# Moving VectorE sums within a fused attention and feed-forward kernel: T4's sums beside batch 1's product with B22, and the sums of w_in spread over the last batch's first products

## The chip, the cores and the metric

One core of one Trainium2 chip. The metric is the device time of one execution in microseconds, here the median of several runs. All runs quoted were fast, with a granted TensorE clock of 0.997 to 1.0. The profile's span is some 1.8 to 2 us shorter than that time; both are given where they are compared.

Engines: PE is TensorE (PEld its weight loads), DVE is VectorE, ACT is ScalarE, SP issues the transfers. A line of the timeline reads: start and length in us, engine, line of the kernel, operation, result<-inputs, shapes, and how many instructions it merges; brackets give the idle time just before it and who ended it. In a list of waits the three numbers are the sum in us, how often, and the longest.

## The reference

```python
def _attn_ref(x, state):                      # x (8, 8, 512, 64), state (8, 8, 32, 64)
    scores = scale * x @ state.T; a = softmax(scores);   xread = a @ state
    scores2 = scale * state @ x.T; a2 = softmax(scores2); sread = a2 @ x
    return concatenate([xread, sread], axis=2)
def _moe_ref(x, w_in, w_out):                 # x: the result above as (4352, 512) tokens
    h = x @ w_in                              # (4352, 2048)
    g = h * (1.0 / (1.0 + np.exp(-1.702 * h)))
    return g @ w_out                          # (4352, 512)
```

(Shortened, the softmax as words.) The 512 x-rows of each of 8 batches are one block of work; the 32 state rows of all batches are gathered and done last, as a block called sr.

## The kernel before

From batch 1 on, the product g @ w_out is done in Strassen's form: seven half-size products in place of eight, at the price of sums and differences on DVE. T1, T2, T3, T4 are differences of the quarters of w_out. Where there is room, some of the seven are split once more, into seven products of eight recorded matmuls each. Each batch carries "hooks": lists of other work (attention of the next batch, sums) that are issued at named places between the products.

One batch, cut to what the argument touches:

```python
product(bank(0), A_of(0, 0), B11, "P1")        # hooks P1a, P1b between and after its halves
... # q1, q2, q4
product(bank(1), A_of(0, 1), B21, "P2")        # hooks P2a, P2b
tt(osb, bank(1), k1); out(0, 0, osb)           # first output block; frees bank 1
... # four subtracts, one correction, hook P2
product(bank(0), S1, T1, "P5")                 # hooks P5a, P5b
strassen_low(..., low2, low_banks(), k2, ...)  # P6: seven small products with T2, hooks P6.1 ...
left3 = sums(0, ...); tt(t01, bank(0), k2)
hook("P6")
left4 = sums(NU, ...)                          # (not in batch 1)
product(bank(3), A_of(0, 1), B22, "P3")        # the product with B22, hooks P3a, P3b
strassen_low(left3, ..., low3, ...)            # P7: seven small products with T3
strassen_low(left4, ..., low4, ...)            # P4: seven small products with T4
                                               # (batch 1: one whole product with T4)
```

Inside the small form three PSUM banks are used in turn, so a product must wait until the add of the product three places earlier has read its bank:

```python
product(o[0], a11, b11);  nc.scalar.copy(p, o[0]);  at(1)
product(o[1], s2, t2);    add(u2, o[1], p);         at(2)
product(o[2], a12, b21);  add(c11, o[2], p);        at(3)
product(o[0], a21, t3);   add(u3, o[0], u2);        at(4)
product(o[1], s1, t1);    ...                       # fifth: needs u2's read of o[1]
```

After batch 1 the sums of T4 were made once and stored, to be loaded by later batches; and the last batch's hooks made the sums for sr (eight of 1024 columns over w_in, four of 256 over the state rows), one per hook:

```python
hooks = {name: [steps[k]] for k, name in enumerate(
    ("P1b", "P2a", "P2", "P5a", "P5b", "P6", "P3a", "P3b", "P7.1", "P7.2", "P7.3", "P7.4"))}
hooks["P3b"].append((low_third, (T2,)))        # restores T2 (gives back a quarter that the small form had turned into a difference); likewise T3 at P4.1, T4 at P4.7
...
strassen_two(b, out_of(b), hooks, a4)
if b == 1:
    t = low4_room()
    for fn, args in low_sums(T4, low4_parts(t)):
        fn(*args)                              # three subtracts of 512 columns
    nc.sync.dma_start(kept4, t)
    low_third(T4)                              # a fourth, in place
```

## Time and profile before

| | before |
|---|---|
| time, median | 738.25 us (738.12 to 738.28, 3 runs) |
| span of the profile | 736.3 us |
| PE busy | 720.9 us (98%) |
| DVE busy | 539.4 us (73%) |
| waits of PE for DVE where the change works | 1.6 us (last batch) and 0.6 us (after batch 1) |

The columns are: window in us, its length, then busy us (and instructions) of PE, PEld, DVE, ACT and POOL, PE's granted clock, DMA share and GB/s.

```profile
155.00:203.00 48.00, 48.00 (x403) 40.59 (x402) 37.47 (x76) 14.40 (x29) 0.00 (x0) 1.00 0.06 23
203.00:240.00 37.00, 36.42 (x176) 31.86 (x175) 23.32 (x38) 12.51 (x20) 0.00 (x0) 1.00 0.28 74
240.00:631.00 391.00, 391.00 (x2860) 340.10 (x2859) 291.41 (x597) 128.68 (x238) 0.00 (x0) 1.00 0.13 36
631.00:660.00 29.00, 29.00 (x163) 26.28 (x162) 21.04 (x33) 2.89 (x6) 0.00 (x0) 1.00 0.11 37
660.00:690.00 30.00, 28.37 (x224) 27.35 (x224) 22.35 (x53) 2.45 (x8) 0.00 (x0) 1.00 0.08 28
```

From 155 to 690 us PE is busy for the whole of every stretch but two: 37.00 - 36.42 = 0.58 us are missing after batch 1, and 30.00 - 28.37 = 1.63 us in the last batch. Between them, over 391 us, nothing is missing.

### The profile page before, as it was taken

The numbers are of one execution on the slowest core, as the hardware profiler recorded it, in microseconds if no ns is written. First come the engines' busy times: TensorE is split into PE (matmuls) and PEld (weight loads), VectorE is DVE, ScalarE is ACT, GpSimd is POOL, SyncE is SP. The second block draws the span as 40 slices with busy tenths as digits, with TensorE's granted clock in tenths as the row PEclk, the third lists the DMA queues.
The fourth block names the chain that finished last, engine by engine and source line by source line (L and its number), as shares of the span: only waits on it lengthen the run. The fifth ranks groups of instructions, "written<-read, shape, count | busy, mean of one in ns | idle before, by whom it ended". The sixth has DMA issues, their size and how long they took to land.

```text
span 736.3 us, 11509 instructions
## 1 busy us (share of the span) xinstructions
PE 720.9 (98%) x4757; PEld 567.4 (77%) x4759; DVE 539.4 (73%) x1077; ACT 233.8 (32%) x430; POOL 0.8 (0%) x8
## 2 busy tenths in 40 slices
PE   7999999999999999999999999999999999999996
PEld 3333444478888789879888789878987988898995
DVE  6997999729766887668867786688667886778440
ACT  4786411033224511432144323341144214200210
POOL 0000000000000000000000000000000000000000
PEclk9999999999999999999999999999999999999999
DMA  9921244010041011300140014001120010010000
GB/s 234 344 93 52 89 162 125 0 58 15 1 121 27 16 35 54 60 1 16 46 102 1 16 45 105 0 16 45 50 55 1 15 62 26 1 58 29 16 1 28
DMA packets 49780, 40.84 MB, mean 55 GB/s; under 512 B 36544, under 2 KB 44224, under 8 KB 49728
## 3 DMA queue, kind: packets, MB, share of 16 engines
q1 hardware_dynamic: 49728, 40.11, 18.5%
q8 instruction: 37, 0.61, 0.3%
q14 instruction: 15, 0.12, 0.1%
HBM read 30.41 MB, written 9.70 MB: 54 GB/s over the span
## 4 chain that ended last, share of the span: by engine, by line
PE 93%; DVE 2%; ACT 2%; DMA 2%; issue 0%; SPq 0%; DVEq 0%; ACTq 0%
PE o L670 27%; PE o L938 16%; PE low L622 10%; PE o L490 8%; PE h L472 7%; PE o L622 6%; PE upx L938 5%; PE M L303 4%; PE o L533 2%; PE xT L282 2%; PE o L303 1%; PE sr L452 1%; PE warm L123 1%; PE upx_sr L938 1%; DMA out_dram<-osb_sr 1%; PE eT L441 1%
## 5 line engine op out<-in xcount | busy, mean ns | idle before, releaser
L670 PE MATMUL o<-w_out,g 128*128 128x256 f32 x672 | 152.7, 381 | 0.0
L948 DVE TENSOR_TENSOR g<-o,g 128x512 f32<-128x512 f32 (+1 forms) x140 | 88.0, 650 | 84.3 <-PE o L938 83.4
L670 PEld LDWEIGHTS o<-w_out,g 128*128 128x128 f32 x672 | 125.2, 190 | 26.2 <-issue 10.5
L945 ACT ACTIVATE g<-g 128x512 f32<-128x512 f32 (+1 forms) x84 | 49.8, 599 | 101.3 <-DVE g L948 101.3
L938 PE MATMUL o<-ta,M 128*128 128x256 f32 x192 | 49.4, 380 | 0.6 <-DVE g L948 0.6
L670 PE MATMUL o<-sums,later 128*128 128x256 f32 x224 | 49.5, 379 | 0.0
L938 PE MATMUL upx<-aT,M 128*128 128x256 f32 x192 | 49.3, 379 | 0.0
L938 PE MATMUL o<-ta,ms 128*128 128x256 f32 x192 | 48.3, 379 | 0.0
L670 PEld LDWEIGHTS o<-sums,later 128*128 128x128 f32 x224 | 42.6, 190 | 5.8
L432 ACT COPY M<-M 128x512 f32<-128x512 f32 x64 | 33.2, 597 | 37.7 <-PE M L303 37.7
L938 PEld LDWEIGHTS o<-ta,M 128*128 128x128 f32 x192 | 36.4, 190 | 5.9 <-DVE g L948 1.0
L938 PEld LDWEIGHTS o<-ta,ms 128*128 128x128 f32 x192 | 36.5, 190 | 5.0
L938 PEld LDWEIGHTS upx<-aT,M 128*128 128x128 f32 x192 | 36.1, 190 | 4.7
L513 DVE TENSOR_TENSOR later<-g,g 128x512 f32<-128x512 f32 (+1 forms) x32 | 20.8, 649 | 17.5 <-ACT g L475 17.5
L303 PE MATMUL M<-w_in,stT 64*32 64x512 f32 x512 | 32.7, 594 | 0.2 <-ACT eT L442 0.2
L622 PE MATMUL low<-low,g 128*128 128x128 f32 x256 | 32.8, 275 | 0.0
L472 PE MATMUL h<-low,M 128*128 128x512 f32 x64 | 29.7, 600 | 1.4 <-DVE low L384 1.4
L622 PEld LDWEIGHTS low<-low,g 128*128 128x128 f32 x256 | 30.7, 192 | 0.0
L629 ACT COPY pu<-o 128x128 f32<-128x128 f32 x13 | 3.4, 265 | 84.6 <-PE o L622 84.6
L472 PE MATMUL h<-aT,M 128*128 128x512 f32 x64 | 28.7, 599 | 1.4 <-ACT M L432 1.4
L625 DVE TENSOR_TENSOR pu<-low,pu 128x128 f32<-128x128 f32 x27 | 7.8, 290 | 29.1 <-PE low L622 29.1
L490 PE MATMUL o<-w_out,g 128*128 128x512 f32 x64 | 28.7, 594 | 0.0
(186 smaller groups left out, 1187.8 us busy)
## 6 DMA issues: line engine op xcount, KB each, us to landing
later<-in_moe_w_out_dram SPq DMA_DIRECT2D x16, 512.0 KB
xn<-in_x_dram SPq DMA_DIRECT2D x28, 256.0 KB
w_out<-in_moe_w_in_dram SPq DMA_DIRECT2D x12, 512.0 KB
low<-low SPq DMA_DIRECT2D x7, 768.0 KB
out_dram<-osb SPq DMA_DIRECT2D x18, 256.0 KB
out_dram<-later SPq DMA_DIRECT2D x14, 256.0 KB
later<-in_moe_w_in_dram SPq DMA_DIRECT2D x4, 512.0 KB
sums<-in_x_dram SPq DMA_DIRECT2D x4, 256.0 KB
```

The costliest lines, as they stand in the source:

```text
L282: nc.tensor.transpose(ps[:, c], x_heads(b, c, j), ident)
L303: nc.tensor.matmul(ps[g][st], A[b]["stT"][rows, st], rhs(rows, j), start=True, stop=True)
L432: nc.scalar.copy(m[:, g], ps[g])
L472: nc.tensor.matmul(hps, lhs[i], rhs[i], start=(i == 0), stop=(i == n - 1))
L490: nc.tensor.matmul(ops, G[key, f // 2][:, f % 2, P * r : P * (r + 1)], w_out[:, f], start=(f == 0), stop=(f == NF - 1))
L513: nc.vector.tensor_tensor(out=s1, in0=a21, in1=a22, op=ALU.add)
L533: nc.tensor.matmul(ps[:, r], lhs[f][:, P * r : P * (r + 1)], rhs[:, f], start=(first and r == 0 and f == 0), stop=(f == HF - 1), skip_grou ...
L622: nc.tensor.matmul(ps, lhs[f], rhs[:, f], start=(f == 0), stop=(f == QF - 1))
L670: nc.tensor.matmul(ps[:, r], lhs[f][:, P * r : P * (r + 1)], rhs[:, f], start=(r == 0 and f == 0), stop=(f == HF - 1), skip_group_check=True,)
L938: nc.tensor.matmul(ps[:, k], lhs[i][:, o : o + P], rhs[i], start=(first and k == 0 and i == 0), stop=(i == n - 1), skip_group_check=True,)
L945: nc.scalar.activation(out=dst, in_=src, func=AF.Gelu_apprx_sigmoid)
L948: nc.vector.tensor_tensor(out=dst, in0=ps, in1=x, op=ALU.add)
```

## The change

Its intent: take DVE work out of the two places where PE waits for DVE, and put it where DVE has idle time. Part A moves T4's three sums to hook P3a of batch 1. Part B deals the twelve sums for sr out anew, seven of the eight long ones ahead of P6, and restores T2 at hook P6.

```diff
+    def low4_make(a):
+        t = low4_room()
+        for fn, args in low_sums(T4, low4_parts(t)):
+            fn(*args)
+        nc.sync.dma_start(kept4, t)
...
-            hooks = {
-                name: [steps[k]]
-                for k, name in enumerate(("P1b", "P2a", "P2", "P5a", "P5b", "P6", "P3a", "P3b", "P7.1", ...))
-            }
-            hooks["P3b"].append((low_third, (T2,)))
+            order = (
+                ("P1b", 1), ("P2a", 4), ("P2", 1), ("P5a", 1), ("P3a", 1), ("P7.1", 1), ("P7.2", 1), ("P7.3", 1), ("P7.4", 1),
+            )
+            ...
+            for name, t in (("P6", T2), ("P4.1", T3), ("P4.7", T4)):
+                hooks[name] = [(low_third, (t,))]
...
+        hooks["P3a"][k:k] = [(low4_load if b > 1 else low4_make, (a4,))]
+        strassen_two(b, out_of(b), hooks, a4 if b > 1 else None)
         if b == 1:
-            t = low4_room()
-            for fn, args in low_sums(T4, low4_parts(t)):
-                fn(*args)
-            nc.sync.dma_start(kept4, t)
             low_third(T4)
```

More of the change, by code (lines that the diff above doesn't have):

```diff
@@ L1130 @@
             steps, left, right = sr_sums()
-            hooks = {
-                name: [steps[k]]
-                for k, name in enumerate(("P1b", "P2a", "P2", "P5a", "P5b", "P6", "P3a", "P3b", "P7.1", "P7.2", "P7.3", "P7.4"))
-            }
-            hooks["P3b"].append((low_third, (T2,)))
-            hooks["P4.1"] = [(low_third, (T3,))]
-            hooks["P4.7"] = [(low_third, (T4,))]
+            order = (
+                ("P1b", 1), ("P2a", 4), ("P2", 1), ("P5a", 1), ("P3a", 1), ("P7.1", 1), ("P7.2", 1), ("P7.3", 1), ("P7.4", 1),
+            )
+            hooks = {}
+            for name, n in order:
+                hooks[name], steps = steps[:n], steps[n:]
+            assert not steps
+            for name, t in (("P6", T2), ("P4.1", T3), ("P4.7", T4)):
+                hooks[name] = [(low_third, (t,))]
         for name, first in ahead.items():
             hooks[name] = first + hooks.get(name, [])
-        a4 = None
-        if b > 1:
-            a4 = {}
-            hooks["P3a"] = hooks.get("P3a", [])
-            k = 3 if b + 1 < B else 0
-            hooks["P3a"].insert(k, (low4_load, (a4,)))
-        strassen_two(b, out_of(b), hooks, a4)
+        a4 = {}
+        k = 3 if b + 1 < B else 0
+        hooks["P3a"][k:k] = [(low4_load if b > 1 else low4_make, (a4,))]
+        strassen_two(b, out_of(b), hooks, a4 if b > 1 else None)
         if b == 1:
-            t = low4_room()
-            for fn, args in low_sums(T4, low4_parts(t)):
-                fn(*args)
-            nc.sync.dma_start(kept4, t)
             low_third(T4)
```

## The prediction

> **What bounds the kernel now.** I read the page first (busy shares, then the chain that ended last), then the list of waits of TensorE alone, then the order of time of PE and DVE around each wait that the change could touch.
>
> ```profile
> span 736.3 us, 11509 instructions
> ...
> PE 720.9 (98%) x4757; PEld 567.4 (77%) x4759; DVE 539.4 (73%) x1077; ACT 233.8 (32%) x430; POOL 0.8 (0%) x8
> ...
> PE 93%; DVE 2%; ACT 2%; DMA 2%; issue 0%; SPq 0%; DVEq 0%; ACTq 0%
> ```
>
> The reader is to see that TensorE (PE) is busy for 98% of the span and makes 93% of the chain. The change removes no matmul, so only PE's holes can shrink: 736.3 - 720.9 = 15.4 us, most of them in the start and the last stores. The list of waits says which holes belong to VectorE (DVE):
>
> ```profile
> PE low L622 <- DVE pu L625: 1.6, 1, 1.6
> PE h L472 <- DVE low L384: 1.4, 1, 1.4
> ...
> PE o L938 <- DVE g L948: 0.6, 1, 0.6
> ```
>
> Two of these lie where the diff works (the L384 one is in the attention prologue). The larger, in order of time on PE and on DVE in the last batch:
>
> ```profile
> 668.61 1.06 PE L622 MATMUL o<-w_out,g 128*128 128x128 f32 x8
> 669.50 1.06 PE L622 MATMUL low<-w_out,g 128*128 128x128 f32 x8
> 672.20 1.16 PE L622 MATMUL low<-low,later 128*128 128x128 f32 x8 [1.63 <-DVE pu L625]
> ```
>
> ```profile
> 655.72 0.29 DVE L625 TENSOR_TENSOR pu<-low,pu 128x128 f32<-128x128 f32 x1 [1.47 <-PE low L622]
> ...
> 664.59 1.22 DVE L901 TENSOR_TENSOR ws<-ws,w_in 128x1024 f32<-128x1024 f32 x1
> ...
> 668.65 1.22 DVE L901 TENSOR_TENSOR w_in<-w_in,w_in 128x1024 f32<-128x1024 f32 x1
> 669.78 1.22 DVE L901 TENSOR_TENSOR ws<-w_in,ws 128x1024 f32<-128x1024 f32 x1
> 670.92 0.68 DVE L1080 TENSOR_TENSOR sums<-sums 128x512 f32<-128x512 f32 x1
> 671.52 0.42 DVE L901 TENSOR_TENSOR ta_sr<-srT 128x256 f32<-128x256 f32 x1
> 671.86 0.28 DVE L625 TENSOR_TENSOR pu<-low,pu 128x128 f32<-128x128 f32 x1
> ```
>
> Seven products of eight small matmuls (P7) follow the product with B22 (P3). The fifth rewrites the PSUM bank of the second, so it needs the small add of 671.86. That add's input was ready near 668.9, but DVE first works off w_in sums, T2's restoring subtract and one srT sum. Earlier, at 655.72, DVE had stood idle for 1.47 us: room in the wrong place. The smaller hole, after batch 1 (DVE):
>
> ```profile
> 195.26 0.69 DVE L837 TENSOR_TENSOR ms<-M 128x512 f32<-128x512 f32 x1 [1.17 <-ACT M L432]
> ...
> 199.59 0.29 DVE L625 TENSOR_TENSOR pu<-low,pu 128x128 f32<-128x128 f32 x1 [2.92 <-PE low L622]
> ...
> 211.51 0.68 DVE L1080 TENSOR_TENSOR low<-sums 128x512 f32<-128x512 f32 x1
> 212.22 1.42 DVE L1080 TENSOR_TENSOR low<-sums,low 128x512 f32<-128x512 f32 x2
> 213.56 0.68 DVE L1080 TENSOR_TENSOR sums<-sums 128x512 f32<-128x512 f32 x1
> 214.16 0.68 DVE L948 TENSOR_TENSOR g<-o,g 128x512 f32<-128x512 f32 x1
> ```
>
> Four operations on T4 stand ahead of the first add of batch 2's up projection; PE resumes at 214.90. Beside P3, at 192 to 199, DVE has 1.17 + 2.92 us idle.
>
> **What the Trainium skill says.** "VectorE: DVE Perf Modes", section on the TRN2 errata of SBUF-source operations, gives an fp32 tensor_tensor of N columns (N+151)/0.96 ns: 1224 for 1024 columns, 691 for 512, 424 for 256, 291 for 128. The trace agrees: 1216 to 1219, 680 to 693, 412 to 425, 287 to 291. So a moved sum costs what it cost before. The same page, "Two Vector instructions with no wait between them", says an instruction that is not held starts before its predecessor is through; here neighbours start 1.13 us apart at 1024 columns and 0.60 at 512, and I count with these distances. "PSUM — Partial Sum Buffer", "Engine vs sequencer instructions", calls VectorE's queue strict FIFO; the 671.86 add, ready since 668.9 and run in turn, agrees. Position in the queue is therefore the whole effect. The same page's rule on bank collisions (guard a bank by semaphores) is why the fifth product must wait for that read.
>
> **The change, part by part.** Each engine has as many instructions as before. PE's and ACT's order is unchanged; only DVE's order changes, and one DMA moves.
>
> Part A, T4 after batch 1. Three subtracts (211.51 to 213.56, 2.05 us) and the store of their result move beside P3, behind the transposes that end near 192.5. There DVE then does 2.05 us of T4, 1.57 of the four ta sums, 1.4 of the two ms sums: 5.0 of the 7.06 us until 199.59. P7's first add is not late, by 2.0 us. At 211.51 only T4's restoring subtract is left (0.60), so DVE is free at 212.1; the add can then start when its product is through. In batch 3 that add starts 2.00 us after the first up matmuls (292.99 against 290.99), here 210.70 + 2.00 = 212.7 instead of 214.16. What PE gains: in batch 3 the product that had to wait starts 294.45 - 290.99 = 3.46 us after the first up matmuls; in batch 2, 214.90 - 210.70 = 4.20. Gain 0.74 us, somewhat more than the idle figure of 0.58, because the restarted matmul is longer too.
>
> Part B, w_in sums in the last batch. Before, five of the eight 1024-column sums precede P6 (the seven small products ahead of P3), one follows it and two stand beside P3. After, seven precede P6 and one follows. Ahead of P6: from 645.60, four sums at 1.13 (s2, hi, s4, s1) bring the first output add from 647.02 to 650.1; it must have freed its bank by 653.67, when P6 begins there: 2.9 us to spare with its 0.7. Then 2.53 us of add, subtracts and correction as now, one sum 1.13, two subtracts 1.2, one sum 1.13: the first P6 add starts at 656.1 instead of 655.72. P6's fifth product starts at 657.24 and, as at 671.86 to 672.20, needs the add to start 0.34 earlier, 656.9: not late, by 0.76 us. The idle 1.47 us is what pays.
>
> Around P3: the sum at 664.59 (1.13) becomes T2's subtract (0.60), so all behind it comes 0.53 earlier: 668.65 becomes 668.12. Then one sum (1.14) and one srT sum (0.34): the add that held PE starts at 669.60 instead of 671.86. It was needed at 670.39 - 0.34 = 670.05, so it is in time by 0.45 us. PE's distance from P7's first product to its fifth is now 672.20 - 666.83 = 5.37 us; in batch 1, without a wait, 201.11 - 197.54 = 3.57. Gain 1.80 us (idle figure: 1.63). The next add, behind another srT sum, starts near 670.1 and is needed near 670.9: also in time.
>
> Behind P7 the order on DVE is the old one, and PE ran without a hole from 672.20 to the end of its work at 730; its adds follow PE. The stores at the end, each waiting for the one before, hang on PE's end and shift along. Sum: 0.74 + 1.80 = 2.54 us; 738.25 - 2.54 = 735.7.
>
> **Rivals.** (1) The wait only moves. Seven sums ahead of P6 could make P6 wait. For it: the idle room there is 1.47 us and the extra work 2.26. Against: the waits of DVE on PE and PE's need leave 0.76 us, as worked out. If I am wrong by a whole sum, 0.4 us of PE time come back: 736.1. (2) P7 still waits, because one w_in sum and one srT sum stay ahead of its add. For it: the slack is the smallest here, 0.45 us. If the idle slot of DVE behind P3 is worth nothing, some 0.5 us remain: 736.2. (3) Part A waits for a buffer: T4's sums go into the room that batch 2's x held, free when its last reader on PE is through (192.06). Even if the wait were for all the attention matmuls up to 193.9, DVE would be through at 199.0, before 199.59: nothing lost. (4) DVE was never the limit at the end and PE's gain vanishes in the final transfers: 738.2. Against: the last stores begin only when DVE has read PE's last products (3.08 us of idle there wait on PE). (5) Another engine order or a slow transfer costs more than 15 us: nothing points to it, as queue bytes and instruction counts stay.
>
> **Range and chances.** Both gains are read from waits that the trace names, with slack behind each. Central 735.7. Low 735.1: both gains full, plus some tenths of run and chip. High 736.7: the larger gain down to half, or rivals 1 and 2 together. Two per cent is 14.8 us; PE's holes in all are 15.4 us and the change touches 2.5, so within 2% has 0.99, and the rest is split.
>
> **What would show it.** The wait of the small products on the small add and the wait of the up projection on its add both leave the list of PE's waits. P7's add in the last batch starts about 2.3 us earlier against the first P7 product, and P7 spans 3.57 us from first product to fifth; the first P6 add sits some 0.4 us later against its product. T4's sums appear near 192.5, and the ms sum near 196 has no idle before it. PE's busy time stays near 721 while the span falls to about 733.8. I would be wrong if a new wait of PE on DVE appears in P6 or P7 of the last batch, if batch 1's P7 starts its adds late, or if the end of the span doesn't follow PE.

## The result, and the profile after

| | before | after |
|---|---|---|
| time, median | 738.26 us (738.12 to 738.4, 4 runs) | 735.39 us (735.31 to 735.41, 4 runs) |
| span | 736.3 us | 733.5 us |
| PE busy | 720.9 us | 720.7 us |
| DVE busy | 539.4 us | 539.5 us |

The ratio of the fast runs is 0.9961, with a 95% interval of 0.9944 to 0.9978: within 2%, yet outside noise. A ratio here is the mean time of one kernel's fast runs over that of the other's of the same rounds, so not quite the ratio of the medians quoted. The difference of the medians is 2.87 us, that of the spans 2.8 us.

The source grew by six lines above the products, so line 622 is now 628, 625 is 631, 901 is 907, 938 is 944, 948 is 954 and 1080 is 1086. The stretches of the changed kernel, as above:

```profile
155.00:203.00 48.00, 48.00 (x404) 40.59 (x403) 39.23 (x79) 14.41 (x29) 0.00 (x0) 1.00 0.10 39
203.00:240.00 37.00, 37.00 (x180) 32.69 (x179) 22.27 (x36) 13.29 (x23) 0.00 (x0) 1.00 0.23 52
...
631.00:660.00 29.00, 29.00 (x163) 26.29 (x162) 23.22 (x36) 2.75 (x5) 0.00 (x0) 1.00 0.12 37
660.00:690.00 30.00, 30.00 (x245) 29.28 (x244) 20.04 (x52) 3.18 (x9) 0.00 (x0) 1.00 0.09 28
```

PE is now busy throughout in both places (37.00 of 37.00 and 30.00 of 30.00). DVE's work has only changed places: 1.8 us more in the stretch to 203, and 2.2 us more in the one to 660, at no cost to PE.

The wait in the last batch, on PE and on DVE after the change:

```profile
668.63 1.06 PE L628 MATMUL low<-w_out,g 128*128 128x128 f32 x8
669.53 1.06 PE L628 MATMUL low<-low,later 128*128 128x128 f32 x8
670.42 1.06 PE L628 MATMUL o<-low,g 128*128 128x128 f32 x8
```

```profile
655.28 0.28 DVE L631 TENSOR_TENSOR pu<-low,pu 128x128 f32<-128x128 f32 x1
...
663.72 0.68 DVE L1086 TENSOR_TENSOR sums<-sums 128x512 f32<-128x512 f32 x1
...
667.25 1.22 DVE L907 TENSOR_TENSOR ws<-w_in,ws 128x1024 f32<-128x1024 f32 x1
668.39 0.42 DVE L907 TENSOR_TENSOR ta_sr<-srT 128x256 f32<-128x256 f32 x1
668.72 0.28 DVE L631 TENSOR_TENSOR pu<-low,pu 128x128 f32<-128x128 f32 x1
```

The fifth small product of P7 (669.53) now follows the fourth by 0.90 us, as in other batches. An add that starts 0.34 us before it would do, as at 671.86 and 672.20 before; it starts at 668.72, in time by 0.47 us. One long sum stands ahead of it where two stood, and the idle 1.47 us ahead of the first P6 add (655.28) are gone: filled with sums.

Batch 1 and what follows it, on PE before, on PE after, and on DVE after:

```profile
214.90 1.13 PE L938 MATMUL o<-ta,M 128*128 128x256 f32 x4 [0.58 <-DVE g L948]
```

```profile
214.13 1.03 PE L944 MATMUL o<-ta,M 128*128 128x256 f32 x4
```

```profile
192.41 0.65 DVE L1086 TENSOR_TENSOR low<-sums 128x512 f32<-128x512 f32 x1
193.09 1.42 DVE L1086 TENSOR_TENSOR low<-sums,low 128x512 f32<-128x512 f32 x2
...
195.89 0.69 DVE L843 TENSOR_TENSOR ms<-M 128x512 f32<-128x512 f32 x1
...
199.57 0.29 DVE L631 TENSOR_TENSOR pu<-low,pu 128x128 f32<-128x128 f32 x1 [2.27 <-PE low L628]
...
211.49 0.68 DVE L1086 TENSOR_TENSOR sums<-sums 128x512 f32<-128x512 f32 x1
212.68 0.69 DVE L954 TENSOR_TENSOR g<-o,g 128x512 f32<-128x512 f32 x1 [0.51 <-PE o L944]
```

The three sums fill what was idle: the 1.17 us ahead of the ms sum are gone, and of the 2.92 us ahead of P7's first add 2.27 are left; that add starts at 199.57, as before. The add after batch 1 (212.68) now waits 0.51 us for PE: the direction of the wait has turned.

### The profile page after: what moved, and what is told of

It is laid out like the page before. It is cut to its first block, busy times and chain, and to the rows that moved or that the text cites. A ratio compares the mean times of both kernels' runs of the same rounds, so it can differ in the third digit from the quotient of the medians.

```text
span 733.5 us, 11513 instructions
## 1 busy us (share of the span) xinstructions
PE 720.7 (98%) x4759; PEld 567.5 (77%) x4759; DVE 539.5 (74%) x1077; ACT 234.1 (32%) x430; POOL 0.8 (0%) x8
## 4 chain that ended last, share of the span: by engine, by line
PE 95%; ACT 2%; DMA 2%; SPq 0%; DVE 0%; issue 0%; DVEq 0%; ACTq 0%
PE o L676 28%; PE o L944 17%; PE low L628 11%; PE o L490 8%; PE h L472 7%; PE o L628 6%; PE upx L944 6%; PE M L303 4%; PE o L533 2%; PE xT L282 2%; PE o L303 1%; PE sr L452 1%; PE warm L123 1%; PE upx_sr L944 1%; DMA out_dram<-osb_sr 1%; PE eT L441 1%
## 5 line engine op out<-in xcount | busy, mean ns | idle before, releaser
L490 PE MATMUL o<-w_out,sums 128*128 128x512 f32 x64 | 28.4, 594 | 0.0
```

What stands on the lines that cost most here:

```text
L490: nc.tensor.matmul(ops, G[key, f // 2][:, f % 2, P * r : P * (r + 1)], w_out[:, f], start=(f == 0), stop=(f == NF - 1))
```

## The experiments

Theory: position in DVE's in-order queue, relative to one add that frees a PSUM bank, is the whole effect; the two holes are independent and add up. Rivals: PE's gain is absorbed later; the amount of work beside P3 counts and not its place; the wait only moves to P6; each sum carries a share of the gain; the end hangs on the transfers. Each edit is against the changed kernel. All kernels gave correct results. The first four ran on one chip in one series (the kernel before: 738.26 us), the last three in another (before: 738.21 us).

### T4's sums alone

The last batch's hooks as before, the rest as in the change (cut):

```diff
-            order = (("P1b", 1), ("P2a", 4), ("P2", 1), ("P5a", 1), ("P3a", 1), ...)
+            hooks = {name: [steps[k]] for k, name in enumerate(("P1b", "P2a", "P2", "P5a", "P5b", "P6", ...))}
```

> Only part A: T4's sums beside batch 1's product with B22, the last batch as before. My theory (two holes, each with its own cause, which add up): the hole after batch 1 closes, worth the start-to-start distance 0.75 us plus 0.10 us for the slower first matmuls of a restarted product, 0.85 us: 737.4 us, and the wait of 1.6 us in the last batch stays. Rival (what PE gains there is lost again in a later stage, because DVE sets the pace of the following batch): 738.3 us.

Measured: 737.28 us (737.24 to 737.37), ratio 0.9987 (interval 0.9975 to 1.0). The gain is 0.98 us by the medians, 0.8 by the spans (736.3 to 735.5). The interval touches 1, so the ratio alone would not settle it; the nine runs of before (738.09 to 738.33) and these five do not overlap, and the list of waits has lost the 0.6 us and kept the 1.6. The gain isn't lost later.

### The w_in sums alone

T4's sums back behind batch 1, the last batch as in the change (cut):

```diff
-        hooks["P3a"][k:k] = [(low4_load if b > 1 else low4_make, (a4,))]
+            hooks["P3a"].insert(k, (low4_load, (a4,)))      # for b > 1 only
         if b == 1:
+            t = low4_room()
+            for fn, args in low_sums(T4, low4_parts(t)):
+                fn(*args)
+            nc.sync.dma_start(kept4, t)
             low_third(T4)
```

> Only part B: the w_in sums spread to the first products of the last batch, T4's sums after batch 1 as before. My theory: the hole of the last batch closes, worth 1.80 + 0.10 = 1.90 us: 736.4 us, and the 0.6 us wait after batch 1 stays. Both parts alone then add up to the 2.8 us of the whole change. Rival (the holes are not independent): clearly another number, and the sum of the two gains is not 2.8 us.

Measured: 736.36 us (736.34 to 736.41), ratio 0.9975 (0.9961 to 0.9988): a gain of 1.90 us, as expected. 0.98 + 1.90 = 2.88 us, and the whole change gained 2.87: the parts add up. Its list of PE's waits for DVE, the prologue aside, has one line left:

```profile
PE o L944 <- DVE g L954: 0.6, 1, 0.6
```

### All eight sums ahead of P6

```diff
-("P2", 1), ("P5a", 1), ("P3a", 1),
+("P2", 1), ("P5a", 2), ("P3a", 0),
```

> The changed kernel with all eight w_in sums ahead of P6 and none beside the product with B22. Theory of position in DVE's queue: the first add of P6 moves from 655.28 to 656.41, but is needed at 656.03 for the fifth P6 product at 656.37: a new wait of PE in P6 of 0.4 us, 0.5 us with the restart: 735.9 us. Rival (what matters is only that few sums are beside the product with B22; the more are moved away the better): 735.4 us or less and no wait.

Measured: 735.99 us (735.84 to 736.11), ratio 0.997 (0.9957 to 0.9982), 0.53 us slower than the changed kernel of the other series (735.46). PE, and the DVE instructions ahead of the add:

```profile
656.73 1.16 PE L628 MATMUL low<-low,g 128*128 128x128 f32 x8 [0.21 <-DVE pu L631]
```

```profile
655.26 1.22 DVE L907 TENSOR_TENSOR ws<-w_in,ws 128x1024 f32<-128x1024 f32 x1
656.40 0.28 DVE L631 TENSOR_TENSOR pu<-low,pu 128x128 f32<-128x128 f32 x1
```

The add starts at 656.40 and P6's fifth product at 656.73, 0.38 us later than its 3.57 us after P6's first (652.78). The rival "the fewer sums beside P3, the better" falls: the same wait appears in P6. The prediction's first rival was real, one sum further on.

### Six sums ahead of P6, two beside the product with B22

```diff
-("P2", 1), ("P5a", 1), ("P3a", 1),
+("P2", 1), ("P5a", 0), ("P3a", 2),
```

> The changed kernel with one of the seven sums ahead of P6 put back beside the product with B22 (six ahead, two beside). Theory of position: the first add of P7 moves from 668.72 to 669.85 and is needed at 669.19: a wait of 0.66 us in P7, 0.76 us with the restart: 736.15 us. If instead the loss were proportional to the work moved (2.26 us of sums gave 1.90 us), one sum of 1.13 us would cost 0.95 us: 736.3 us. Rival (the amount of DVE work in the batch, not its place): 735.4 us.

Measured: 736.17 us (736.12 to 736.43), ratio 0.9973 (0.996 to 0.9985), 0.71 us slower than the changed kernel. On PE:

```profile
668.60 1.06 PE L628 MATMUL low<-w_out,g 128*128 128x128 f32 x8
670.14 1.16 PE L628 MATMUL low<-low,later 128*128 128x128 f32 x8 [0.49 <-DVE pu L631]
```

DVE's work in the batch is the same, so amount is not what counts. The times can't tell the 0.76 us of slack and restart (736.15) from the 0.95 us of a proportional share (736.3), as both lie within the spread of the runs. The trace can: P7's fifth product comes 4.22 us after its first (665.92) in place of 3.57, and the next one 1.00 us after it in place of 0.89, together 0.76 us. With one sum more or less ahead of P6 PE waits: of the splits tried, seven and one alone showed no wait in P6 or P7.

### Only one of T4's three sums moved

```diff
     def low4_make(a):
-        t = low4_room()
-        for fn, args in low_sums(T4, low4_parts(t)):
-            fn(*args)
-        nc.sync.dma_start(kept4, t)
+        a["t"] = low4_room()
+        fn, args = low_sums(T4, low4_parts(a["t"]))[0]
+        fn(*args)
...
         if b == 1:
+            for fn, args in low_sums(T4, low4_parts(a4["t"]))[1:]:
+                fn(*args)
+            nc.sync.dma_start(kept4, a4["t"])
```

> The changed kernel with only the first of T4's three sums beside the product with B22; two stay after batch 1. Theory of slack: the first add of batch 2's up projection starts near 213.43 (212.68 in the changed kernel, 214.16 before) and is needed near 213.39, so nearly all of part A's gain is there: 735.4 to 735.55 us. Rival (each of the three sums carries a third of the 0.85 us): 735.95 us.

Measured: 735.68 us (735.54 to 735.98), ratio 0.9966 (0.9953 to 0.9978), against 735.46 us (735.35 to 735.61) of the changed kernel in the same series: 0.22 us slower. The runs scatter by 0.4 us, so the median lies outside what I expected and the lowest inside. The trace is sharper. On PE, then on DVE:

```profile
214.20 1.13 PE L943 MATMUL o<-ta,M 128*128 128x256 f32 x4
215.17 1.03 PE L943 MATMUL upx<-aT,M 128*128 128x256 f32 x4
```

```profile
213.46 0.69 DVE L953 TENSOR_TENSOR g<-o,g 128x512 f32<-128x512 f32 x1
```

The add starts at 213.46 (expected 213.43), and the product that needs it at 214.20, only 0.01 us behind its place (3.47 us after the first up matmuls at 210.73, where 3.46 is undisturbed), but its four recorded matmuls take 0.97 us to the next start in place of 0.87. So one sum of three bought all but 0.1 us in this trace, where equal shares would have left 0.57 us; that rival (735.95) falls by the trace and the median, though not by the slowest run (735.98). The store of T4's sums stayed after batch 1 here, so its earlier place in the change is not what gave the gain.

### Own rooms for the last four output blocks

This answers the question whether the end hangs on PE. The last four blocks are stored from one shared room, so each must wait for the store before it. The last two adds of the changed kernel:

```profile
724.87 0.42 DVE L552 TENSOR_TENSOR osb_sr<-o,g 128x256 f32<-128x256 f32 x1 [3.45 <-DMA out_dram<-osb_sr]
728.73 0.42 DVE L552 TENSOR_TENSOR osb_sr<-o,g 128x256 f32<-128x256 f32 x1 [3.43 <-DMA out_dram<-osb_sr]
```

By then the rooms of T2's and T3's sums are no longer needed:

```diff
-            o = opool.tile([P, nb, HN], FP32, tag="osb", name=f"osb_{key}_{i}{k}")
+            o = low[:, 2 * i + k, : nb * HN].rearrange("p (r n) -> p r n", n=HN)
```

> The changed kernel, but each of the last four output blocks gets its own room (free by then) in place of one shared room, so no final add waits for the store before it. If the end hangs on PE as far as the last product, and after it on one add and one store, the last add starts 3.71 us after its product, at 727.91 in place of 728.73: 0.82 us less, 734.6 us, faster than both kernels. Rival (stores are in each other's way, the queue is the limit at the end): 735.4 us.

Measured: 734.61 us (734.34 to 734.63), ratio 0.995 (0.9937 to 0.9962): 0.85 us faster than the changed kernel of the same series, and the fastest of all kernels here. The same adds now wait for PE alone:

```profile
724.31 0.43 DVE L552 TENSOR_TENSOR low<-o,g 128x256 f32<-128x256 f32 x1 [2.97 <-PE o L533]
727.76 0.43 DVE L552 TENSOR_TENSOR low<-o,g 128x256 f32<-128x256 f32 x1 [3.03 <-PE o L533]
```

The stores were not in each other's way; the shared room was. It cost 0.85 us and not the 3.45 + 3.43 us of the two waits, because PE's last products ran meanwhile: with own rooms each of these adds waits some 3 us for PE.

### The changed kernel again

> The changed kernel once more, as the yardstick of this series: 735.4 us, and a ratio to the kernel before of 0.996.

Measured: 735.46 us (735.35 to 735.61), ratio 0.9962 (0.9948 to 0.9975).

### One measure for all traces

The scatter of the runs can be left out by taking, in each trace, the distance from batch 2's first up matmuls to the start of PE's last product (before: 210.70 to 726.97). What the start of a run adds or saves doesn't enter.

| kernel | distance, us | against the changed kernel |
|---|---|---|
| before | 516.27 | 2.75 |
| T4's sums alone | 515.41 | 1.89 |
| w_in sums alone | 514.36 | 0.84 |
| changed, and changed again | 513.52 | 0 |
| eight ahead | 513.99 | 0.47 |
| six ahead | 514.27 | 0.75 |
| one of T4's three sums moved | 513.64 | 0.12 |
| own rooms | 513.52 | 0 |

So T4's sums are worth 0.86 us and the w_in sums 1.91 (516.27 less their own distance), against 0.85 and 1.90 expected, and the one long sum too many costs 0.47 and 0.75 us, against 0.5 and 0.76. Own rooms leave it as it was: their gain is at the end alone. The move of T2's restoring subtract was not tried by itself; P7's add comes 2.27 us earlier, and the two long sums that no longer stand ahead of it make 2.26, so nothing is left for it.

## Why the prediction was right

**Which holes.** Right. The prediction took the gain from two waits of PE on DVE and nothing else. Both are gone from the list, no new one came, and each part alone removes its own. That the product waits for the add is in the traces (672.20 behind 671.86); of the bank rule that the prediction gives as the reason no run here shows more, as none breaks it.

**Part A.** DVE's times came as worked out: T4's sums at 192.41 (near 192.5), P7's first add not late, the add after batch 1 at 212.68 (212.7). The feared wait for the x room didn't come: no idle stands before the first T4 sum.

**Part B.** The first P6 add starts 2.48 us after P6's first product (655.28 - 652.80) where it started 2.05 (655.72 - 653.67), so 0.43 later as against "some 0.4". P7's add starts 2.76 us after P7's first product (668.72 - 665.96) in place of 5.03 (671.86 - 666.83): 2.27 earlier, "about 2.3". P7 runs 3.57 us from first product to fifth, the figure given.

**The term that was too small.** The sum was 2.54 us and the measured gain 2.87, so each gain was slightly undersized. I had taken start-to-start distances up to the product that waited, not through it. A product that resumes after a wait also runs 0.10 us longer: before, 214.90 to the next group's start at 215.87 is 0.97 us, after, 214.13 to 215.00 is 0.87; in the last batch 0.99 (672.20 to 673.19) against 0.89 (669.53 to 670.42). With it the gains are 0.85 and 1.90 us, 2.75 in all, and PE is 673.19 - 670.42 = 2.77 us earlier behind the second hole; that stays to its last product (726.97 against 724.20, 2.77). The remaining 0.1 us to the medians' 2.87 is within the spread of the runs (0.28 us for the kernel before).

The prediction did name the longer product, but as the reason why its 0.74 us exceed the idle figure of 0.58. That step is wrong: a distance that ends at the product's start cannot hold its length. The 0.16 us are overlap. Undisturbed, a product starts before the recorded end of the one ahead of it (214.13 against 213.27 + 1.03 = 214.30), and a wait loses this too. So the idle time that the profile shows, 0.58 + 1.63 = 2.21 us, understates what the two waits cost by some 0.17 us of overlap and 0.10 us of restart each: 2.75 us.

Why a resumed product is slower was not tried. The traces fit a first weight load that is no longer done ahead: it starts 0.01 us before its product after the wait (672.19 and 672.20), and 0.11 us before it undisturbed (669.42 and 669.53).

**The rivals.** The wait that only moves to P6 is real, but begins at eight sums, not at seven: the slack left at seven is 656.37 - 0.34 - 655.28 = 0.75 us (predicted 0.76, though the prediction's own rounded terms, 656.9 - 656.1, give 0.8). The slack in P7 is the smallest, as predicted, 0.47 us (0.45), and one sum more there exceeds it. The rival that the end hangs on transfers falls: PE's gain reached the end whole. The prediction's sentence that the last stores shift along was right; it saw that each waits for the one before, but not that this costs some 0.85 us.

## What to carry to other kernels

When the bound engine waits for a helper that is idle elsewhere, find the one instruction it waits for and count what stands ahead of it in the helper's in-order queue; the slack of that instruction, in us, tells how much more may stand there; what stayed under it cost PE nothing here. Moving more was no better: one sum too many ahead of P6 brought a wait of the same kind. A wait cost more than the idle time that the profile shows for it (2.75 us for 2.21 shown), so measure it from start to start, through the product that waited. And look at the last stores of a kernel: a buffer shared by outputs can be paid for at the end, here with 0.85 us.

## What the Trainium skill lacked or had wrong

- "TensorE: Matmul & The Clock Gate" (its sections on single matmul latency and the back-to-back issue gap) has no cost for a stream of matmuls that resumes after a wait: here the first product after one took some 0.1 us longer, in the two waits before, and in the three experiments that had a late add (1.00 us in place of 0.89 with eight or six sums ahead, 0.97 in place of 0.87 with one of T4's sums moved).
- No page that I looked up gives the time from a VectorE add that frees a PSUM bank to the matmul that waits for it: here 0.34 us from the add's start (671.86) to the matmul's (672.20), for a 128-column add of 0.28 us, and 0.33 us with eight or six sums ahead (656.40 and 656.73, 669.81 and 670.14).
